# Matmuls grouped by tile shape in a three-stage kernel, with the float64 conversion ending in GpSimd's add, four input buffers for it and a single decay buffer

## The chip, the core and the metric

The kernel runs on one core of a Trainium2 chip. The core has a matrix engine (TensorE, PE in the profile; PEld is its weight load), VectorE (DVE), ScalarE (ACT), GpSimd (POOL) and SyncE (SP), which here issues nearly all DMAs. Each engine takes its own instructions in their order and waits on semaphores for the others. The metric is device time in microseconds (us), the median of several runs.

## The reference

Three computations run one after the other. The first is a linear attention with decay, for 4 batches, 8 heads, 768 steps and a head size of 48:

```python
for t in range(S):
    cur = np.einsum('bhd,bhe->bhde', u[None] * kt, vt)
    y[:, :, t] = np.einsum('bhd,bhde->bhe', rt, state + cur)
    state = wt[:, :, :, None] * state + np.einsum('bhd,bhe->bhde', kt, vt)
```

Its output, as 3072 tokens of width 384, goes through a soft mixture of experts (8 experts of 4 slots, width 1024). That takes a softmax of `x @ phi` over the tokens to fill the slots, two matmuls with a relu between them in each expert, and a softmax over the slots to hand the results back. The last part is bilinear:

```python
a = x @ w_a
b = x @ w_b
return (a * b @ w_out).astype(np.float32)
```

The three matrices `w_a`, `w_b` (384x1536) and `w_out` (1536x384) are float64, and the kernel turns them into float32 itself. The inputs r, k, v, w, u, phi, w1 and w2 are float32.

## The kernel before, in words

**Units.** The attention is cut into chunks of 128 steps. A unit is three chunks of four heads (two pairs of heads), and there are 16 units (`NU`). A unit n has three parts, each a generator. `front` turns w, k and r so that the head dimension lies on the partitions (PE transposes, L508, and ACT copies, L513 and L515). It forms the running products of the decays forwards (`decays`, a DVE scan, L532) and backwards (`backward`, L537), sums up decays over 1 for a later range check (`over`, ACT, L546), and multiplies them into k and r (`key` on GpSimd, L551; `query` on DVE, L555; `own` on GpSimd, L558). `mid` forms the scores within a chunk (`scores`, L581, one call for a head pair p and a head hh of it, masked by DVE at L584), turns the keys back (`keys`, L592), and forms the state updates (`updates`, L600 on PE, L605 to L611 on DVE), the states (GpSimd, L621) and the bonus term. `out` adds up in PSUM (the matmul accumulators, in banks) what the earlier chunks' state gives (L674, 128x128 weights) and what the scores give (L678, weights of 128x64), and DVE adds the bonus (L683).

**What sets the order.** The order is written by the program. `run_all` interleaves generators: each yields a share of its planned time, and the one that is furthest behind its plan goes next. In round n it interleaves `mid(n)`, `front(n + 1)`, `out(n - 1)`, half a token group of the experts' softmax (`moe.group`), a piece of the float64 conversion (`convert`) and one to two loads of expert weights. `MIDS` and `FRONTS` are lists of steps with their shares. Every engine then runs its own part in that order.

**Conversion.** 36 pieces of 128x384 float64 are loaded as pairs of 32-bit words into `cv_raw` buffers (three of them before). ACT turns both words of a piece into partial results (`stage`, L706 and L707), DVE shifts the upper one (L714), GpSimd adds the lower one as integers (L717), and DVE merges the sign, which it takes from the raw upper word (L720). The load three pieces on goes into the same buffer and waits for that.

**Buffers and queues.** The natural-order inputs have fixed buffers: w two, k and r one, v three. A load of the next unit's data is issued by SP when the last reader has its turn in the program. For w that is `over`. Score tiles are taken from the same ring of five PSUM banks as transposes and updates (`TPB`, tag `tp`). SP issues its DMAs in order, and each waits for a free one of eight semaphores as well as for the readers of its buffer.

**After the units** the experts run (L806, L831), for which 16 weight tiles are loaded: 4 early, the others into buffers that the attention gives back. Then come the bilinear part as products of slot pairs (L966) and the output (L1101, L1104).

The functions that the diff touches and what calls them:

## Time and profile before

| what | value |
|---|---|
| median of 3 runs | 411.43 us (408.06 to 414.76) |
| the profiled execution's own time | 412.5 us |
| its span, from the first to the last instruction | 410.8 us |
| mean granted TensorE clock over the span | 0.935 of full speed |
| units (first forward scan to the end of the last `out`) | 7.7 to about 268 us |
| experts, waiting for their weights | about 275 to 302 us |
| bilinear part and output | about 306 to 410 us |

The profile is of one execution. PE rows are matmuls, which are pipelined, so a row's length includes its fill and drain, and the distance from one row's start to the next tells more than its length. A float32 matmul stands as two instructions, a transpose as one. Tile shapes stand as rows*columns of the weights: 64*128 uses half of the array's rows, 128*64 half of its columns.

### The profile page before, as it was taken

How to read it: one execution, taken by the hardware profiler on the slowest of the kernel's cores; microseconds unless marked ns; L12 is line 12 of the kernel's file. 1: busy time of each engine (PE TensorE's matmuls, PEld its weight loads, DVE VectorE, ACT ScalarE, POOL GpSimd, SP SyncE). 2: the span in 40 equal slices, each digit the busy share in tenths (PEclk: the TensorE clock that was granted, in tenths of full speed). 3: DMA queues.
4: the chain of work that ended last, by engine and by line, in shares of the span. 5: the costliest groups of instructions: out<-in, count | busy, mean ns of one | idle time of the engine just before them, and what ended most of it. 6: DMA issues, size and time to landing. Idle time of an engine off the chain costs nothing.

```text
span 410.8 us, 9983 instructions
## 1 busy us (share of the span) xinstructions
PE 383.2 (93%) x3634; PEld 300.3 (73%) x3634; DVE 305.3 (74%) x616; ACT 233.9 (57%) x672; POOL 182.2 (44%) x225
## 2 busy tenths in 40 slices
...
GB/s 139 144 199 153 171 134 204 205 132 230 221 137 193 183 166 193 201 195 145 151 186 98 123 274 282 167 307 375 375 128 219 102 0 0 164 295 291 135 99 65
...
## 3 DMA queue, kind: packets, MB, share of 16 engines
...
q8 instruction: 31, 0.51, 0.5%
...
## 4 chain that ended last, share of the span: by engine, by line
PE 31%; DVE 9%; DMA 8%; issue 4%; ACT 2%; POOL 1%; SPq 1%; ACTq 0%; POOLq 0%; DVEq 0%
DMA s<-in_moe_w_dram 6%; PE yo L1101 5%; PE tp L581 4%; PE y L678 3%; PE yo L1104 3%; PE tp L966 3%; PE y L674 3%; PE tp L508 2%; DMA out_dram<-s 2%; DVE s L532 1%; PE tp L203 1%; DVE s L941 1%; PE tp L600 1%; DVE s L952 1%; PE misc L214 1%
## 5 line engine op out<-in xcount | busy, mean ns | idle before, releaser
L581 PE MATMUL tp<-s,s 64*128 64x128 f32 x384 | 64.9, 306 | 0.4 <-DVE s L611 0.3
L581 PEld LDWEIGHTS tp<-s,s 64*128 64x128 f32 x384 | 52.0, 203 | 9.1 <-issue 2.0
L508 PE MATMUL tp<-ident,s 128*128 128x128 f32 x288 | 52.2, 304 | 4.4 <-ACT s L513 3.2
L584 DVE TENSOR_TENSOR s<-tp,s 128x384 f32<-128x384 f32 x64 | 35.1, 549 | 19.9 <-PE tp L581 19.6
L551 POOL TENSOR_TENSOR s<-s,s 128x384 f32<-128x384 f32 x30 | 38.7, 1308 | 17.4 <-DVE s L537 14.8
L648 ACT ACTIVATE s<-s,s 128x48 f32<-128x48 f32 x192 | 46.2, 323 | 0.3
L678 PE MATMUL y<-s,s 128*64 128x48 f32 x768 | 44.8, 241 | 0.0
L508 PEld LDWEIGHTS tp<-ident,s 128*128 128x128 f32 x288 | 35.0, 152 | 12.8 <-ACT s L513 3.5
L558 POOL TENSOR_TENSOR s<-s,s 128x384 f32<-128x384 f32 x32 | 35.5, 1128 | 17.9 <-DVE s L555 17.9
L532 DVE TENSOR_TENSOR_SCAN s<-s,s 128x387 f32<-128x387 f32 x32 | 38.4, 1240 | 6.4 <-ACT s L513 6.4
L678 PEld LDWEIGHTS y<-s,s 128*64 128x64 f32 x768 | 32.5, 146 | 12.7 <-issue 6.0
L717 POOL TENSOR_TENSOR wab<-wab,s 128x384 int32<-128x384 int32 x24 | 28.5, 1188 | 25.0 <-issue 7.3
L1101 PE MATMUL yo<-s,s 128*128 128x384 f32 x192 | 37.8, 338 | 0.5 <-DVE s L1066 0.4
L966 PE MATMUL tp<-s,s 128*128 128x384 f32 x144 | 29.8, 358 | 5.2 <-DVE s L952 4.4
L1101 PEld LDWEIGHTS yo<-s,s 128*128 128x128 f32 x192 | 33.8, 188 | 1.2 <-DVE s L1066 1.1
L515 ACT ACTIVATE s<-tp 128x384 f32<-128x384 f32 x64 | 30.7, 491 | 5.8 <-PE tp L508 5.2
L966 PEld LDWEIGHTS tp<-s,s 128*128 128x128 f32 x144 | 26.0, 198 | 9.9 <-DVE s L952 6.9
L674 PE MATMUL y<-s,s 128*128 128x96 f32 x128 | 30.4, 321 | 0.0
L537 DVE TENSOR_TENSOR_SCAN s<-s,s 128x387 f32<-128x387 f32 x32 | 29.1, 952 | 0.5
L1108 ACT ACTIVATE s<-yo 128x384 f32<-128x384 f32 x24 | 11.8, 492 | 28.1 <-PE yo L1105 14.8
L621 POOL TENSOR_TENSOR s<-s,pc_all 64x288 f32<-64x288 f32 (+1 forms) x32 | 20.5, 640 | 14.1 <-DVE s L611 12.9
L674 PEld LDWEIGHTS y<-s,s 128*128 128x128 f32 x128 | 20.5, 201 | 7.7 <-issue 4.1
...
## 6 DMA issues: line engine op xcount, KB each, us to landing
...
s<-in_w_dram SPq DMA_DIRECT2D x48, 96.0 KB, 2.9
s<-in_k_dram SPq DMA_DIRECT2D x48, 96.0 KB, 3.2
s<-in_r_dram SPq DMA_DIRECT2D x48, 96.0 KB, 2.9
s<-in_v_dram SPq DMA_DIRECT2D x48, 96.0 KB, 3.3
...
```

The costliest lines, as they stand in the source:

```text
L508: nc.tensor.transpose(out=pt[:, c, :], in_=t[:, c, 2 * p:2 * p + 2, :].rearrange("p h d -> p (h d)"), identity=ident)
L515: nc.scalar.activation(out=(kT if nm == "k" else rT)[:, off:off + 3 * C], in_=pt.rearrange("p c s -> p (c s)"), func=ACTF.Copy)
L532: nc.vector.tensor_tensor_scan(out=P[:, hs[p]], data0=wt[:, hs[p]], data1=self.lo, initial=0.0, op0=ALU.mult, op1=ALU.max)
L551: (nc.gpsimd if n else nc.vector).tensor_tensor(out=part(suf, p, 1), in0=part(suf, p, 1), in1=plain(kT, p), op=ALU.mult)
L558: nc.gpsimd.tensor_tensor(out=plain(rT, p), in0=plain(rT, p), in1=plain(kT, p), op=ALU.mult)
L581: nc.tensor.matmul(out=ap_[:, c, :], lhsT=K[64 * hh:64 * hh + 64, o + 1:o + 1 + C], rhs=R[64 * hh:64 * hh + 64, o:o + C], start=True, stop ...
L584: nc.vector.tensor_tensor(out=a, in0=ap_, in1=self.mask.unsqueeze(1).to_broadcast([128, 3, C]), op=ALU.mult)
L648: nc.scalar.activation(out=av[:, c, h], in_=V[:, c, h, 0:D], func=ACTF.Copy, scale=a0[:, c, h // 2, h % 2:h % 2 + 1])
L674: nc.tensor.matmul(out=yp[:, c].rearrange("p h d -> p (h d)"), lhsT=R[:, o:o + C], rhs=self.sbd[q][:, p, (j + 2) % 3, :], start=True, stop ...
L678: nc.tensor.matmul(out=yp[th, c, hh, :], lhsT=am[p, hh][:, c, th], rhs=V[:, c, 2 * p + hh, :], start=j == 0, stop=j == 0 or hh == 1)
L966: nc.tensor.matmul(out=tp[m], lhsT=a[:, m * 128:(m + 1) * 128], rhs=b, start=first and i == 0, stop=last and i == 2)
L1101: nc.tensor.matmul(out=y, lhsT=a[:, m, :], rhs=self.th[:, m, :], start=m == 0 and a is fh, stop=False)
```

## The change

The diff makes these edits:

1. `scores` takes a pair of heads at once: two PSUM tiles, and the six matmuls alternate between the heads, whose operands lie on partitions 0 to 63 and 64 to 127. The two masks follow.
2. `out` issues the state's matmuls of both head pairs first (both PSUM tiles are open at once), then twelve score matmuls for each pair in one row.
3. `MIDS` puts the two `keys` together and the two `updates` together, and shifts shares.
4. The conversion: DVE first cuts the raw upper word to its sign bit in place, then shifts and merges the sign in one instruction, and GpSimd's integer add is last. `stage` runs one piece further ahead. There are four raw buffers, and the load into one waits for GpSimd's add.
5. w has one buffer, `over` writes in place, and loads w for the next unit (before: the one after the next). The buffer set free is the fourth raw buffer.
6. A branch that the constant `YDVE` had switched off is gone.

```diff
-YDVE = 1
-MIDS = (('keys', (0,), 327), ('scores', (0, 0), 654), ('bonus_t', (), 440), ('keys', (1,), 327),
-        ('scores', (0, 1), 654), ('updates', (0,), 474), ('scores', (1, 0), 0), ('bonus', (), 95),
-        ('updates', (1,), 544), ('av', (0,), 257), ('states', (), 0), ('av', (1,), 327), ('scores',
-        (1, 1), 0), ('av', (3,), 327), ('av', (2,), 327))
+MIDS = (('keys', (0,), 0), ('keys', (1,), 400), ('scores', (0,), 900), ('bonus_t', (), 700), ('updates', (0,), 0),
+        ('updates', (1,), 1018), ('bonus', (), 95), ('scores', (1,), 654), ('av', (0,), 257), ('states', (), 0),
+        ('av', (1,), 327), ('av', (3,), 327), ('av', (2,), 327))
...
-        for nm, nb in (("w", 2), ("k", 1), ("r", 1), ("v", 3)):
+        for nm, nb in (("w", 1), ("k", 1), ("r", 1), ("v", 3)):
...
-        self.load("w", 1)
...
         def over():
-            t = rT.bitcast(BF16)[:, 0:12 * 64]
-            nc.scalar.activation(out=t, in_=self.nat["w"][n % 2].rearrange("p c h d -> p (c h d)"),
-                                 func=ACTF.Relu, bias=self.neg1, accum_out=self.wover[:, n:n + 1])
-            self.load("w", n + 2)
+            t = self.nat["w"][0].rearrange("p c h d -> p (c h) d")[:, :, 0:self.sh.D]
+            nc.scalar.activation(out=t, in_=t, func=ACTF.Relu, bias=self.neg1, accum_out=self.wover[:, n:n + 1])
+            self.load("w", n + 1)
...
-        def scores(p, hh):
-            ap_ = ps_a.tile([128, 3, C], F32, tag="A", name="ap_")
+        def scores(p):
+
+            aps = [ps_a.tile([128, 3, C], F32, tag="A", name="ap_") for hh in range(2)]
             for c in range(3):
                 o = (p * 3 + c) * (C + 1)
-                nc.tensor.matmul(out=ap_[:, c, :], lhsT=K[64 * hh:64 * hh + 64, o + 1:o + 1 + C],
-                                 rhs=R[64 * hh:64 * hh + 64, o:o + C], start=True, stop=True)
...
+                for hh in range(2):
+                    nc.tensor.matmul(out=aps[hh][:, c, :], lhsT=K[64 * hh:64 * hh + 64, o + 1:o + 1 + C],
+                                     rhs=R[64 * hh:64 * hh + 64, o:o + C], start=True, stop=True)
...
+        yps = [ps_y.tile([128, 3, 2, D], F32, tag="y", name="yp") for p in range(2)]
+        cs = [c for c in range(3) if hf * 3 + c]
         for p in range(2):
-            yp = ps_y.tile([128, 3, 2, D], F32, tag="y", name="yp")
+            for c in cs:
+                o = (p * 3 + c) * (C + 1)
+                nc.tensor.matmul(out=yps[p][:, c].rearrange("p h d -> p (h d)"), lhsT=R[:, o:o + C],
+                                 rhs=self.sbd[q][:, p, (hf * 3 + c + 2) % 3, :], start=c == cs[0], stop=False)
+        yield 1084
+        for p in range(2):
+            yp = yps[p]
             for c in range(3):
...
                 for hh in range(2):
                     for th in (slice(0, 64), slice(64, 128)):
                         nc.tensor.matmul(out=yp[th, c, hh, :], lhsT=am[p, hh][:, c, th],
-                                         rhs=V[:, c, 2 * p + hh, :], start=j == 0, stop=j == 0 or hh == 1)
-                yield 542
+                                         rhs=V[:, c, 2 * p + hh, :], start=False, stop=c == 2 and hh == 1)
...
-def f64_to_f32(nc, out, raw, ahead):
-
-
-    bits = out.bitcast(I32)
-    nc.vector.tensor_scalar(out=out.bitcast(U32), in0=out.bitcast(U32), scalar1=3, scalar2=None,
-                            op0=ALU.logical_shift_left)
+def f64_to_f32(nc, out, raw):
+
+
+    bits = out.bitcast(U32)
+    nc.vector.tensor_scalar(out=raw[:, :, 1], in0=raw[:, :, 1], scalar1=0x80000000, scalar2=None, op0=ALU.bitwise_and)
     yield 1
-    nc.gpsimd.tensor_tensor(out=bits, in0=bits, in1=raw[:, :, 0].bitcast(I32), op=ALU.add)
-    ahead()
-    yield 2
-    nc.vector.scalar_tensor_tensor(out=out.bitcast(U32), in0=raw[:, :, 1], scalar=0x80000000, in1=out.bitcast(U32),
-                                   op0=ALU.bitwise_and, op1=ALU.bitwise_or)
+    nc.vector.scalar_tensor_tensor(out=bits, in0=bits, scalar=3, in1=raw[:, :, 1], op0=ALU.logical_shift_left,
+                                   op1=ALU.bitwise_or)
+    yield 1
+    nc.gpsimd.tensor_tensor(out=out.bitcast(I32), in0=out.bitcast(I32), in1=raw[:, :, 0].bitcast(I32), op=ALU.add)
     yield 1
```

**On PE, in the second half of a unit.** Names: `tp`, `y` and `misc` are PSUM tiles, `s_6_92` and the like are areas of on-chip memory, and the line numbers of the changed kernel are 1 to 3 lower at these places (L581 becomes L579, L600 becomes L599, L678 becomes L680). Before, the scores of a head and the pieces of `out` stand between other steps:

```order
L581 MATMUL tp_1460<-s_6_92,s_4_85 128x128 x3
L674 MATMUL y_1411<-s_6_92,s_4_86 128x96
L678 MATMUL y_1411<-s_4_87,s_8_95 64x48 x4
L508 MATMUL tp_1471<-ident,s_3_80 128x128 x3
L600 MATMUL tp_1486<-s_6_92,s_5_91 64x48 x6
L674 MATMUL y_1411<-s_6_92,s_4_86 128x96
L678 MATMUL y_1411<-s_4_87,s_8_95 64x48 x4
L581 MATMUL tp_1504<-s_6_92,s_4_85 128x128 x3
L639 MATMUL tp_1509<-ident,s_5_89 128x128
L640 MATMUL tp_1509<-ident,s_5_89 128x64
L600 MATMUL tp_1513<-s_6_92,s_5_91 64x48 x6
```

The same place in the changed kernel:

```order
L599 MATMUL tp_1458<-s_6_92,s_5_91 64x48 x6
L599 MATMUL tp_1467<-s_6_92,s_5_91 64x48 x6
L505 MATMUL tp_1476<-ident,s_3_80 128x128 x3
L680 MATMUL y_1411<-s_4_87,s_8_95 64x48 x12
L638 MATMUL tp_1507<-ident,s_5_89 128x128
L639 MATMUL tp_1507<-ident,s_5_89 128x64
L579 MATMUL tp_1512<-s_6_92,s_4_85 128x128
L579 MATMUL tp_1513<-s_6_92,s_4_85 128x128
L579 MATMUL tp_1512<-s_6_92,s_4_85 128x128
L579 MATMUL tp_1513<-s_6_92,s_4_85 128x128
L579 MATMUL tp_1512<-s_6_92,s_4_85 128x128
L579 MATMUL tp_1513<-s_6_92,s_4_85 128x128
```

Updates stand side by side, the score part of `out` is one row of twelve, and the two heads' score matmuls alternate between two PSUM tiles.

**On DVE, at the start of a unit.** Before, the shift of a piece stands ahead of the unit's forward scans (a scan is printed here as SCALAR_TENSOR_TENSOR of 128x387), and the sign of the piece behind the backward scans, with GpSimd's add between the two:

```order
L584 TENSOR_TENSOR s_8_94<-tp_2017,s_6_92 128x384
L714 TENSOR_SCALAR wo<-wo 128x384
L532 SCALAR_TENSOR_TENSOR s_3_82<-s_2_77,s_3_83 128x387 x2
L541 RECIPROCAL s_2_78<-s_3_82 128x6
L537 SCALAR_TENSOR_TENSOR s_4_85<-s_2_77,s_2_78 128x387 x2
L720 SCALAR_TENSOR_TENSOR wo<-s_1_73,wo 128x384
L584 TENSOR_TENSOR s_8_94<-tp_2094,s_6_92 128x384
```

In the changed kernel:

```order
L714 SCALAR_TENSOR_TENSOR wab_182<-wab_182,s_1_73 128x384
L266 SCALAR_TENSOR_TENSOR acc<-acc,s_7_93,misc_1949 96x384
L583 TENSOR_TENSOR s_8_94<-tp_2010,s_6_92 128x384
L583 TENSOR_TENSOR s_8_94<-tp_2011,s_6_92 128x384
L712 TENSOR_SCALAR s_1_74<-s_1_74 128x384
L529 SCALAR_TENSOR_TENSOR s_3_82<-s_2_77,s_3_83 128x387 x2
L714 SCALAR_TENSOR_TENSOR wab_182<-wab_182,s_1_74 128x384
L538 RECIPROCAL s_2_78<-s_3_82 128x6
L534 SCALAR_TENSOR_TENSOR s_4_85<-s_2_77,s_2_78 128x387 x2
```

Two masks now stand between a piece's last DVE step (L714), which GpSimd's add waits for, and the scans, and no DVE step stands behind that add.

**On SP, in the first half of a unit.** Before, the w buffers alternate (`s_1_72` here, `s_2_76` in the unit after), and a raw load, ahead of the k loads, waits for DVE:

```order
L727 DMA s_1_75<-in_moe_w_b_dram 128x768 [waits DMAHW5_49,DVE_49]
L492 DMA s_2_79<-in_k_dram 128x4x48 [waits DMAHW6_49,PE_49]
L492 DMA s_2_79<-in_k_dram 128x4x48 [waits DMAHW7_49,PE_49]
L492 DMA s_2_79<-in_k_dram 128x4x48 [waits DMAHW0_49,PE_49]
L307 DMA ct_176<-cstage 48x384 [waits DMAHW1_49,Activation_49]
L492 DMA s_1_72<-in_w_dram 128x4x48 [waits DMAHW2_49,Activation_49]
L492 DMA s_1_72<-in_w_dram 128x4x48 [waits DMAHW3_49]
L492 DMA s_1_72<-in_w_dram 128x4x48 [waits DMAHW4_49]
```

In the changed kernel:

```order
L723 DMA s_1_74<-in_moe_w_b_dram 128x768 [waits DMAHW1_49,Pool_49]
L773 DMA s_10_1170<-in_moe_w_dram 128x3x256 [waits DMAHW2_49]
L489 DMA s_2_79<-in_k_dram 128x4x48 [waits DMAHW3_49,PE_49]
L489 DMA s_2_79<-in_k_dram 128x4x48 [waits DMAHW4_49,PE_49]
L489 DMA s_2_79<-in_k_dram 128x4x48 [waits DMAHW5_49,PE_49]
L305 DMA ct_172<-cstage 48x384 [waits DMAHW6_49,Activation_49]
L489 DMA s_2_76<-in_w_dram 128x4x48 [waits DMAHW7_49,Activation_49]
L489 DMA s_2_76<-in_w_dram 128x4x48 [waits DMAHW0_49]
L489 DMA s_2_76<-in_w_dram 128x4x48 [waits DMAHW1_49]
```

The raw load waits for GpSimd, and the w loads, in the same place, are for the next unit.

## Rows read from the trace of the kernel before

**Rows 1.** The page, busy time of each engine over the span.

```profile
PE 383.2 (93%) x3634; PEld 300.3 (73%) x3634; DVE 305.3 (74%) x616; ACT 233.9 (57%) x672; POOL 182.2 (44%) x225
```

**Rows 2.** Windows of the span: length, busy time by engine, granted clock, DMA share, GB/s.

```profile
63.90:109.80 45.90, 45.28 (x521) 35.47 (x520) 41.23 (x88) 36.79 (x116) 30.20 (x31) 1.00 0.78 190
...
141.90:173.20 31.30, 30.61 (x350) 23.61 (x349) 29.30 (x63) 24.13 (x79) 20.44 (x21) 1.00 0.78 190
173.20:179.90 6.70, 5.71 (x60) 4.58 (x57) 6.63 (x10) 4.02 (x11) 4.38 (x4) 1.00 0.95 221
179.90:193.60 13.70, 13.09 (x78) 10.24 (x78) 10.16 (x26) 7.83 (x25) 7.02 (x8) 0.50 0.65 165
...
224.10:237.40 13.30, 13.22 (x147) 10.44 (x146) 10.31 (x24) 8.07 (x28) 6.40 (x7) 1.00 0.47 105
237.40:265.00 27.60, 27.60 (x333) 21.27 (x332) 17.18 (x48) 15.15 (x56) 7.15 (x11) 1.00 0.75 238
...
278.00:302.00 24.00, 24.00 (x298) 10.82 (x297) 9.92 (x26) 8.79 (x21) 0.51 (x1) 1.00 1.00 352
```

**Rows 3.** Timeline of PE within the units: start, length, operation, tile shape, count.

```profile
157.89 0.63 PE L629 MATMUL tp<-s,s 128*32 128x128 f32 x12
...
160.77 0.46 PE L674 MATMUL y<-s,s 128*128 128x96 f32 x2
161.17 0.44 PE L678 MATMUL y<-s,s 128*64 128x48 f32 x8
161.53 0.55 PE L508 MATMUL tp<-ident,s 128*128 128x128 f32 x3
162.01 0.56 PE L600 MATMUL tp<-s,s 128*64 128x48 f32 x12
...
163.60 0.93 PE L581 MATMUL tp<-s,s 64*128 64x128 f32 x6
164.47 0.33 PE L639 MATMUL tp<-ident,s 128*128 128x128 f32 x1
...
169.86 0.49 PE L508 MATMUL tp<-ident,s 128*128 128x128 f32 x3
...
171.14 0.88 PE L508 MATMUL tp<-ident,s 128*128 128x128 f32 x6
```

**Rows 4.** The chain that ended last, PE at 183 us: start, length, what.

```profile
183.43 1.58 PE tp L581 x6
```

**Rows 5.** Groups of DVE instructions by shape: count, busy, mean of one, idle before.

```profile
L532 DVE TENSOR_TENSOR_SCAN s<-s,s 128x387 f32<-128x387 f32 x32 | 38.4, 1240 | 6.4 <-ACT s L513 6.4
...
L720 DVE SCALAR_TENSOR_TENSOR wab<-s,wab 128x384 uint32<-128x384 uint32 x24 | 20.3, 845 | 6.8 <-POOL wab L717 5.1 <-DMA s<-in_moe_w_b_dram 1.4
...
L714 DVE TENSOR_SCALAR wab<-wab 128x384 uint32<-128x384 uint32 x24 | 11.2, 465 | 4.3 <-ACT wab L706 4.3
...
L720 DVE SCALAR_TENSOR_TENSOR wo<-s,wo 128x384 uint32<-128x384 uint32 x12 | 10.0, 831 | 1.9 <-POOL wo L717 1.9
```

**Rows 6.** Timeline of DVE at two units' starts.

```profile
141.93 2.60 DVE L532 TENSOR_TENSOR_SCAN s<-s,s 128x387 f32<-128x387 f32 x2
...
144.79 1.82 DVE L537 TENSOR_TENSOR_SCAN s<-s,s 128x387 f32<-128x387 f32 x2
...
156.93 0.56 DVE L720 SCALAR_TENSOR_TENSOR wab<-s,wab 128x384 uint32<-128x384 uint32 x1 [0.30 <-POOL wab L717]
...
173.22 2.58 DVE L532 TENSOR_TENSOR_SCAN s<-s,s 128x387 f32<-128x387 f32 x2
```

**Rows 7.** Timeline of GpSimd at the first of those starts.

```profile
142.15 1.55 POOL L717 TENSOR_TENSOR wab<-wab,s 128x384 int32<-128x384 int32 x1 [1.92 <-ACT s L513]
```

**Rows 8.** Timeline of SP's DMA issues within a unit.

```profile
161.96 1.99 SPq L492 DMA_DIRECT2D s<-in_w_dram  x3
```

**Rows 9.** DMA issues of 60 to 224 us: count, KB each, median us to landing.

```profile
s<-in_w_dram SPq DMA_DIRECT2D x30, 96.0 KB, 2.8
```

**Rows 10.** Waits of SP's queue: us in total, times, longest.

```profile
SPq L727 <- DVE s L683: 40.6, 11, 5.0
```

**Rows 11.** The chain that ended last, at the experts' weights.

```profile
278.26 8.00 DMA s<-in_moe_w_dram
```

More of the change, by code (lines that the diff above doesn't have):

```diff
@@ L412 @@
 class Chunked:
[L415 removed]
+    AREAS = (((("cv_raw", 768, 1),), (("cv_raw", 768, 1),), (("cv_raw", 768, 1),), (("cv_raw", 768, 1),)),
              ((("nat_w", 768, 1),), (("wt", 775, 1),), (("dl", 774, 1),), (("nat_k", 768, 1),)),
@@ L575, in mid @@
         kn = {}
-        def scores(p, hh):
-            ap_ = ps_a.tile([128, 3, C], F32, tag="A", name="ap_")
+        def scores(p):
+            aps = [ps_a.tile([128, 3, C], F32, tag="A", name="ap_") for hh in range(2)]
             for c in range(3):
                 o = (p * 3 + c) * (C + 1)
-                nc.tensor.matmul(out=ap_[:, c, :], lhsT=K[64 * hh:64 * hh + 64, o + 1:o + 1 + C],
-                                 rhs=R[64 * hh:64 * hh + 64, o:o + C], start=True, stop=True)
-            a = sb.tile([128, 3, C], F32, tag="am", name="am")
-            nc.vector.tensor_tensor(out=a, in0=ap_, in1=self.mask.unsqueeze(1).to_broadcast([128, 3, C]),
-                                    op=ALU.mult)
-            am[p, hh] = a
+                for hh in range(2):
+                    nc.tensor.matmul(out=aps[hh][:, c, :], lhsT=K[64 * hh:64 * hh + 64, o + 1:o + 1 + C],
+                                     rhs=R[64 * hh:64 * hh + 64, o:o + C], start=True, stop=True)
+            for hh in range(2):
+                a = sb.tile([128, 3, C], F32, tag="am", name="am")
+                nc.vector.tensor_tensor(out=a, in0=aps[hh], in1=self.mask.unsqueeze(1).to_broadcast([128, 3, C]),
+                                        op=ALU.mult)
+                am[p, hh] = a
         def keys(p):
```

34 lines of the change are left out of this document (12 added, 22 removed).

## The prediction

> **What bounds the kernel now.** I read the page's busy times first, then the windows by stage, then PE's timeline inside a unit, and last the groups of DVE, GpSimd and SP. The page has PE at 93% of the span and DVE at 74% [rows 1], which would make it a matter of PE alone. The windows say otherwise for the units. Five units at full clock (three from 63.9 us, two from 141.9 us; a unit counts from one pair of forward scans to the next, as from 141.93 on [rows 6]) take 77.2 us, with 75.89 us of PE and 70.53 us of DVE [rows 2]. That is 15.4 us per unit, PE 15.2, DVE 14.1. PE is the bound, and DVE comes only 1.1 us behind it. From 224.1 us on, where no conversion is left, PE is busy 13.22 of 13.30 us and then 27.60 of 27.60, with DVE at 10.31 and 17.18 [rows 2]: there PE is the bound alone. Behind that, from 278 to 302 us, the DMA engines are full (share 1.00, 352 GB/s [rows 2]), and the chain waits for expert weights [rows 11].
>
> A unit at reduced clock costs more: from 179.9 to 193.6 us the granted clock is 0.50 (1.2 of 2.4 GHz), PE is busy 13.09 of 13.70 us [rows 2], and six score instructions take 1.58 us [rows 4] where they take 0.93 at full clock [rows 3].
>
> **The change on PE, per unit.** All by starts and lengths of [rows 3].
> - Scores. Six instructions (three float32 matmuls of 64*128) take 0.87 us from their start at 163.60 to the next row's at 164.47, and there are four such groups. Afterwards two groups of twelve alternate between the halves of the rows. No row shows two row halves at once. The nearest are column tiles: twelve instructions of 128*32 with 128 columns take 0.63 us, where six of 64*128 with as many columns take 0.93, so small tiles of one shape do run side by side. If the halves do so too, twelve cost what six do, and 2 x 0.87 = 1.74 us go. If not, only what a group costs beyond its instructions goes: one more instruction of 128 columns costs 0.11 us (six transposes 0.88, three 0.55), so 0.87 - 6 x 0.11 = 0.21 twice, 0.42 us. I take 1.74, since the 128*32 row is the nearest in kind.
> - Score part of `out`. Eight instructions take 0.44 us and twelve (L600, same tile shape) 0.56, so one costs 0.03. A group of eight is 0.36 us from start to start (161.17 to 161.53); 24 are then 0.36 + 16 x 0.03 = 0.84. Six groups at 0.36 become two at 0.84: 0.48 us less.
> - State part of `out`. A lone pair is 0.40 us (160.77 to 161.17). A unit has six or four pairs, 2.40 or 1.60 us. In a row they are 0.40 + 10 x 0.11 = 1.50 or 0.40 + 6 x 0.11 = 1.06: 0.90 or 0.54 less, 0.72 on average.
> - The two updates side by side save one group's fixed part, 0.36 - 8 x 0.03 = 0.12 us. The keys save less than that and aren't counted.
>
> Together 3.06 us (1.74 without overlapping halves). PE falls from 15.2 to 12.1 us per unit (13.4). Either is below DVE's 14.1: in the units with conversion the next limit is DVE, and whether the halves overlap hardly matters there.
>
> **The change on DVE and GpSimd.** The counts stay: 36 pieces, each with two DVE steps and one add.
> - The wait of the sign step for GpSimd (5.1 + 1.9 = 7.0 us [rows 5]) goes, 0.5 us in each of 14 units. It is idle time, 0.5 of the 1.3 us per unit in which DVE is not busy. Some of the rest is waiting for PE; I leave 0.6.
> - The cut to the sign bit reads and writes every second word, where the shift (465 ns [rows 5]) was dense. No row shows this. Nearest below is that 465 ns; above, an unhindered two-input step over the same strided words, 0.56 us [rows 6]: 0 to 0.1 us per piece, 0.25 us per unit. I take 0, as it is the same operation with one input, and keep 0.25 for the range.
> - GpSimd's add and DVE's scans hinder each other. Two forward scans take 2.60 us where the two backward ones take 1.82 [rows 6], and GpSimd's add started at 142.15 us and ran for 1.55, in the middle of them [rows 7]. Over 32 scans the excess is 38.4 - 16 x 1.82 = 9.3 us [rows 5, 6], some 12 units of 0.78. In the new order two masks stand between the DVE step that releases the add and the scans, so this collision mostly goes; but the other conversion steps now lie at the scans of other units. I count half, 0.39 us per unit (ends 0 and 0.78).
>
> DVE then needs 14.1 - 0.4 = 13.7 us, and with 0.6 idle a unit lasts 14.3 instead of 15.4: 1.1 us less. GpSimd's add is now last, and on POOL's queue `key`, `own` and the states stand behind it; it has 9 to 10 us of work in 15.4 [rows 2], which covers this. If that cover fails, `key` is late, and the next unit's keys with it.
>
> *The shared port.* GpSimd's time (20.44 us in the two units from 141.9 [rows 2]) and the scans without hindrance (2 x 3.64 [rows 6]) and six sign steps at 0.56 add up to 31.1 of 31.3 us. The Trainium skill ("GPSIMD Engine Reference", Key points) says that GpSimd shares its SBUF interfaces with VectorE and is in contention with DVE instructions that have two SBUF inputs. The trace agrees in kind (2.60 against 1.82 us); how strictly no row tells, since GpSimd's lengths hold its own waiting. This is a rival below.
>
> **Loads of w.** They are issued from 161.96 to 163.95 us [rows 8], land 2.8 us later [rows 9], at 166.8, and are for the unit after next. Now the next unit needs them, whose w transposes start at 169.86 [rows 3]: 3.1 us to spare, 2.0 in a shorter unit. ACT's `over`, which the loads wait for, covers fewer elements. Cost 0 while that holds.
>
> **The sum.** From 63.9 to 224.1 us stand ten units, eight of them at full clock: 8 x 1.1 = 8.8 us. For the two at half clock, PE's saving counts 1.58 / 0.87 = 1.8 fold, some 2 us each after DVE's limit; PE's new waits will bring further falls of the clock, and I set the two against each other. At the start the second unit's w comes later (it was loaded at once), while two units at half clock gain: 0. Unit 14 (224.1 to 237.4) goes from 13.3 to DVE's 10.3 + 0.6: 2.4 us. The last stretch (27.6 us, all PE) holds one `mid` and two `out`s: 1.74 + 0.12 + 2 x 1.20 = 4.3 us. But the expert weights follow, and DMA was only 25% free in that stretch, so I count half, 2.1 us. In all 13.3 us. The profiled execution took 412.5 us, so 399.2; the median of the runs lies 1.1 us lower: **398 us**.
>
> **Rivals.**
> 1. *DVE is relieved altogether*: all collisions go, idle falls to 0.4. A unit is 14.1 - 0.78 + 0.4 = 13.7 us, 8 x 1.7, with 4 us from the slow-clock units, 2.4 and 4.3: 24 us, 387. For it: the masks now stand between. Against: GpSimd's `key` still falls on the backward scans. Chance 0.11.
> 2. *The shared port is the bound*: by the 31.1 of 31.3 us nothing is left in the units with conversion, and only the last 4.5 us are gained: 407. Against: DVE's stalls are already inside its 14.1 us. Chance 0.13.
> 3. *The clock falls more often*. It fell at 179.9 us, after a stretch in which PE was busy 5.71 of 6.70 us [rows 2], 85%; afterwards PE has 12.1 of 14.3, also 85%. A spell of 13.7 us at half clock does 7.6 us of the unit's 12.1, so that unit takes 13.7 + 4.5 = 18.2. If half of the eight get one, 4 x 3.9 = 15.6 us are lost again: 413. Against: in most units PE's waits lie apart. Chance 0.11. The Trainium skill ("TensorE: Matmul & The Clock Gate", HAM oscillation) says that gaps in PE's work bring the clock to half, and that each return is paid for; by that rule the time is this rival's, and the trace agrees at 179.9 us.
> 4. *Slower: w comes late.* SP issues in order; a raw load that waits for GpSimd's add stands ahead of the k and w loads. Such loads waited for DVE 11 times, 40.6 us in all, at most 5.0 [rows 10]. From a block of 3.1 us on, the unit is longer than before; with 5.0 the transposes start 3.0 us late in a unit of 14.3, 17.3 us: 8 x 1.8 = 14 us more, less the last 4.5: 422. Against: only some blocks stand ahead of w. Chance 0.10.
> 5. *The row halves don't overlap*, so the change does not do what it says. In the units DVE bounds anyway; the last units gain some 3 us less: 401. Chance 0.07.
>
> **How the numbers follow.** The forecast has 0.48 (391 to 405), the rest as above. About 2% either way, 8.2 us, is what a measurement of this kernel can tell from no change. Faster by over 2% (below 403.2): nine tenths of the forecast, rival 1, most of 5: 0.61. Slower by over 2%: most of 4 and some of 3, 0.11. Within: 0.28. The range 386 to 412 leaves out half of rival 1 and most of 3 and 4.
>
> **What would show it.** In the changed profile: starts of two score instructions of different halves within a few ns, and twelve in about 0.9 us; PE below 90% and DVE above 95% busy in the units; no DVE wait for the add; forward scan pairs near 1.82 us in most units; units of 14.3 us; no PE wait for w. I am wrong if the units keep 15.4 us with DVE below its limit, if PE waits for w or for GpSimd's `key`, or if the half clock covers more of the units than now.

## The result, and the profile after

The changed kernel takes **392.19 us** (median of 4 runs, 391.67 to 393.63), the kernel before 411.54 us (median of 4, 408.06 to 414.76). The ratio is **0.9537, 95% interval 0.9492 to 0.9582**: faster by 4.6%. The profiled execution took 391.77 us with a span of 390.0. Runs of one kernel with the old matmuls differ by some 2.6% among themselves, together with the granted clock; medians are of all runs, ratios of the undisturbed ones.

The page of the changed kernel, busy time of each engine, beside [rows 1]:

```profile
PE 336.3 (86%) x3634; PEld 265.6 (68%) x3634; DVE 308.2 (79%) x616; ACT 227.5 (58%) x672; POOL 181.2 (46%) x224
```

PE's busy time fell by 46.9 us, DVE's did not fall: it rose by 2.9. The windows of the changed kernel (length, then busy time by engine, granted clock, DMA share, GB/s), beside [rows 2]. The first five lines and the last two follow one another; the line of 60.60 to 207.10 holds ten units.

```profile
60.60:102.80 42.20, 37.08 (x499) 28.86 (x497) 41.40 (x86) 32.80 (x108) 29.94 (x31) 1.00 0.88 203
102.80:131.70 28.90, 24.68 (x326) 19.92 (x325) 28.43 (x59) 22.45 (x75) 17.38 (x21) 0.94 0.85 188
131.70:162.10 30.40, 26.64 (x331) 21.39 (x329) 28.79 (x61) 22.22 (x74) 20.78 (x21) 0.89 0.84 190
162.10:191.30 29.20, 24.91 (x328) 19.84 (x328) 28.68 (x60) 22.63 (x76) 17.41 (x21) 0.94 0.86 191
191.30:220.70 29.40, 25.32 (x328) 20.41 (x327) 28.74 (x62) 21.40 (x74) 20.84 (x21) 0.94 0.81 187
...
60.60:207.10 146.50, 126.49 (x1637) 101.01 (x1635) 142.79 (x296) 111.64 (x366) 95.59 (x103) 0.94 0.85 191
...
220.70:255.00 34.30, 29.50 (x413) 22.51 (x415) 21.16 (x67) 17.44 (x69) 7.17 (x12) 0.95 0.83 262
255.00:282.00 27.00, 27.00 (x346) 12.34 (x335) 10.89 (x30) 9.75 (x23) 0.73 (x2) 1.00 1.01 356
```

Over the ten units DVE is busy 142.79 of 146.50 us, 97%, and PE 126.49, 86%: DVE is the bound, PE waits. A unit lasts 14.65 us on average. The same ten units of the kernel before took 160.20 us, with 155.41 of PE, 142.64 of DVE and a clock of 0.94:

```profile
63.90:224.10 160.20, 155.41 (x1656) 122.10 (x1654) 142.64 (x299) 118.36 (x372) 100.56 (x105) 0.94 0.74 178
```

Where the 20.8 us of span came from, by the starts of the forward scans:

| stretch | before | after | gained | forecast |
|---|---|---|---|---|
| start to the fifth unit | 63.9 | 60.6 | 3.3 | 0 |
| ten units | 160.2 | 146.5 | 13.7 | 8.8 |
| unit 14 | 13.3 | 13.6 | -0.3 | 2.4 |
| rest | 173.4 | 169.3 | 4.1 | 2.1 |

PE's rows in two units of the changed kernel (start, length, operation, tile shape, count), beside [rows 3]:

```profile
163.73 0.91 PE L599 MATMUL tp<-s,s 128*64 128x48 f32 x24
164.57 0.55 PE L505 MATMUL tp<-ident,s 128*128 128x128 f32 x3
165.04 0.91 PE L680 MATMUL y<-s,s 128*64 128x48 f32 x24
165.88 0.33 PE L638 MATMUL tp<-ident,s 128*128 128x128 f32 x1
...
168.75 0.90 PE L579 MATMUL tp<-s,s 64*128 64x128 f32 x10 [2.06 <-DVE s L610]
...
174.19 0.94 PE L579 MATMUL tp<-s,s 64*128 64x128 f32 x12
175.06 0.88 PE L505 MATMUL tp<-ident,s 128*128 128x128 f32 x6
...
176.10 1.48 PE L672 MATMUL y<-s,s 128*128 128x96 f32 x12
177.50 0.63 PE L628 MATMUL tp<-s,s 128*32 128x128 f32 x12
```

Twelve score instructions take 0.87 us from their start to the next row's, what six took before: the row halves do run side by side. The score part of `out` takes 0.84 us per pair, as worked out, the state part 1.40 (worked out 1.50). And PE waits for DVE, 2.06 us up to 168.75.

DVE's groups of the changed kernel (count, busy, mean ns of one, idle before), beside [rows 5] and two more of the kernel before, which stand last (L537 is the backward scan, L555 is `query`):

```profile
L534 DVE TENSOR_TENSOR_SCAN s<-s,s 128x387 f32<-128x387 f32 x32 | 35.0, 1121 | 0.5
L529 DVE TENSOR_TENSOR_SCAN s<-s,s 128x387 f32<-128x387 f32 x32 | 33.1, 1072 | 7.0 <-ACT s L510 7.0
...
L712 DVE TENSOR_SCALAR s<-s 128x384 uint32<-128x384 uint32 x36 | 23.2, 644 | 2.9 <-ACT wab L704 2.9
L551 DVE TENSOR_TENSOR s<-s,s 128x384 f32<-128x384 f32 x32 | 20.2, 669 | 0.0
L714 DVE SCALAR_TENSOR_TENSOR wab<-wab,s 128x384 uint32<-128x384 uint32 x24 | 18.2, 760 | 0.1
...
L537 DVE TENSOR_TENSOR_SCAN s<-s,s 128x387 f32<-128x387 f32 x32 | 29.1, 952 | 0.5
L555 DVE TENSOR_TENSOR s<-s,s 128x384 f32<-128x384 f32 x32 | 17.4, 580 | 0.1
```

The forward scans (L529) fell from 38.4 to 33.1 us, but the backward ones (L534) rose from 29.1 to 35.0, `query` (L551) from 17.4 to 20.2, and the cut to the sign bit (L712) takes 644 ns on average where the shift took 465 (456 over all 36 pieces). DVE's wait for GpSimd's add is gone (0.1 us before L714).

### The profile page after: what moved, and what is told of

It reads as the page before. It is cut to its first block, busy times and chain, and to the rows that moved or that the text cites. A ratio compares the mean times of both kernels' runs of the same rounds, so it can differ in the third digit from the quotient of the medians.

```text
span 390.0 us, 9985 instructions
## 1 busy us (share of the span) xinstructions
PE 336.3 (86%) x3634; PEld 265.6 (68%) x3634; DVE 308.2 (79%) x616; ACT 227.5 (58%) x672; POOL 181.2 (46%) x224
## 4 chain that ended last, share of the span: by engine, by line
DVE 49%; PE 24%; DMA 13%; issue 6%; SPq 4%; ACT 3%; POOL 0%; DVEq 0%; ACTq 0%; POOLq 0%
DMA s<-in_moe_w_dram 8%; DVE s L534 8%; DVE s L529 7%; PE yo L1098 6%; DVE s L583 6%; DVE s L712 5%; DVE wab L714 4%; DVE s L551 3%; PE yo L1101 3%; SPq L489 3%; DVE wo L714 2%; PE tp L579 2%; DVE s L683 2%; PE tp L963 2%; PE y L680 2%
## 5 line engine op out<-in xcount | busy, mean ns | idle before, releaser
L505 PE MATMUL tp<-ident,s 128*128 128x128 f32 x288 | 50.0, 298 | 7.7 <-ACT s L593 3.8
L579 PE MATMUL tp<-s,s 64*128 64x128 f32 x384 | 37.2, 298 | 18.9 <-DVE s L610 9.5
L579 PEld LDWEIGHTS tp<-s,s 64*128 64x128 f32 x384 | 30.2, 197 | 24.0 <-issue 21.7
L554 POOL TENSOR_TENSOR s<-s,s 128x384 f32<-128x384 f32 x32 | 37.4, 1190 | 18.5 <-DVE s L551 18.5
L505 PEld LDWEIGHTS tp<-ident,s 128*128 128x128 f32 x288 | 33.5, 148 | 18.1 <-issue 6.0
L583 DVE TENSOR_TENSOR s<-tp,s 128x384 f32<-128x384 f32 x64 | 32.4, 545 | 9.4 <-PE tp L579 9.2
L529 DVE TENSOR_TENSOR_SCAN s<-s,s 128x387 f32<-128x387 f32 x32 | 33.1, 1072 | 7.0 <-ACT s L510 7.0
L534 DVE TENSOR_TENSOR_SCAN s<-s,s 128x387 f32<-128x387 f32 x32 | 35.0, 1121 | 0.5
L680 PEld LDWEIGHTS y<-s,s 128*64 128x64 f32 x768 | 29.0, 156 | 9.0 <-issue 8.7
L680 PE MATMUL y<-s,s 128*64 128x48 f32 x768 | 33.2, 243 | 0.0
L1106 POOL DMA_DIRECT2D out_dram<-s x18 | 9.9, 553 | 33.9 <-ACT s L1105 32.0
L712 DVE TENSOR_SCALAR s<-s 128x384 uint32<-128x384 uint32 x36 | 23.2, 644 | 2.9 <-ACT wab L704 2.9
```

The costliest lines, as they stand in the source:

```text
L505: nc.tensor.transpose(out=pt[:, c, :], in_=t[:, c, 2 * p:2 * p + 2, :].rearrange("p h d -> p (h d)"), identity=ident)
L529: nc.vector.tensor_tensor_scan(out=P[:, hs[p]], data0=wt[:, hs[p]], data1=self.lo, initial=0.0, op0=ALU.mult, op1=ALU.max)
L534: nc.vector.tensor_tensor_scan(out=suf[:, hs[p]][:, ::-1], data0=wt[:, o + 1:o + H + 1][:, ::-1], data1=d1[:, hs[p]][:, ::-1], initial=0.0 ...
L554: nc.gpsimd.tensor_tensor(out=plain(rT, p), in0=plain(rT, p), in1=plain(kT, p), op=ALU.mult)
L579: nc.tensor.matmul(out=aps[hh][:, c, :], lhsT=K[64 * hh:64 * hh + 64, o + 1:o + 1 + C], rhs=R[64 * hh:64 * hh + 64, o:o + C], start=True, ...
L583: nc.vector.tensor_tensor(out=a, in0=aps[hh], in1=self.mask.unsqueeze(1).to_broadcast([128, 3, C]), op=ALU.mult)
```

## The experiments

Each is compared with the kernel before, run on the same chip. The ten units are those from the fifth unit's first forward scan to the fifteenth's, in each kernel's own profile, in us. The experiments ran on several chips, on which the medians of the kernel before are up to 2.3 us apart, so a difference of that size between two experiments counts only where the traces show it too.

| kernel | median | ratio, 95% interval | ten units | PE | DVE | clock |
|---|---|---|---|---|---|---|
| before | 411.5 to 413.8 | | 160.2 | 155.4 | 142.6 | 0.94 |
| changed | 392.19 | 0.9537, 0.9492 to 0.9582 | 146.5 | 126.5 | 142.8 | 0.94 |
| grouping alone | 411.12 | 0.9971, 0.9903 to 1.0038 | 165.1 | 132.4 | 141.6 | 0.90 |
| conversion and buffers alone | 402.98 | 0.9855, 0.9766 to 0.9944 | 146.3 | 145.1 | 143.5 | 1.00 |
| heads in turn | 392.95 | 0.9610, 0.9498 to 0.9723 | 147.6 | 134.1 | 142.7 | 0.93 |
| no add | 376.80 | 0.9198, 0.9110 to 0.9285 | 134.8 | 121.7 | 130.4 | 0.96 |
| old order | 404.43 | 0.9815, 0.9763 to 0.9868 | 155.6 | 131.3 | 134.8 | 0.90 |
| sign a piece later | 402.97 | 0.9782, 0.9730 to 0.9834 | 154.4 | 131.2 | 141.3 | 0.90 |
| sign at the piece's end | 402.57 | 0.9747, 0.9669 to 0.9824 | 157.0 | 131.2 | 148.0 | 0.88 |
| the same, old matmuls | 416.38 | 1.0111, 1.0026 to 1.0196 | 157.9 | 152.3 | 144.7 | 0.95 |
| w early | 389.01 | 0.9457, 0.9408 to 0.9505 | 145.5 | 126.7 | 142.4 | 0.94 |
| sign by ScalarE | 380.36 | 0.9208, 0.9167 to 0.9249 | 138.5 | 123.4 | 130.0 | 0.98 |

**Grouping alone.** The functions `f64_to_f32`, `convert` and `over` and the w buffers are those of before:

```diff
-        for nm, nb in (("w", 1), ("k", 1), ("r", 1), ("v", 3)):
+        for nm, nb in (("w", 2), ("k", 1), ("r", 1), ("v", 3)):
...
-    nc.vector.scalar_tensor_tensor(out=bits, in0=bits, scalar=3, in1=raw[:, :, 1], op0=ALU.logical_shift_left,
-                                   op1=ALU.bitwise_or)
-    yield 1
-    nc.gpsimd.tensor_tensor(out=out.bitcast(I32), in0=out.bitcast(I32), in1=raw[:, :, 0].bitcast(I32), op=ALU.add)
+    nc.gpsimd.tensor_tensor(out=bits, in0=bits, in1=raw[:, :, 0].bitcast(I32), op=ALU.add)
+    ahead()
+    yield 2
+    nc.vector.scalar_tensor_tensor(out=out.bitcast(U32), in0=raw[:, :, 1], scalar=0x80000000, in1=out.bitcast(U32),
+                                   op0=ALU.bitwise_and, op1=ALU.bitwise_or)
```

> The changed kernel with the conversion, the w buffers and over() of before: only the grouping of matmuls (scores, out, MIDS) is left of the change. Theory (PE's grouping makes the gain, VectorE is the next limit): VectorE needs about 13.9 us per unit as before and still waits 0.5 us for GpSimd's add, so units of 14.6 to 15.0 us and a time of 391 to 399 us. Rival (the new order of the conversion carries at least half of the gain): 401 us or more.

The rival's side: 411.12 us, no gain that can be measured, although PE needs 23 us less in the ten units. Its waits of DVE from 60 to 224 us (us in total, times, longest):

```profile
DVE wab L720 <- POOL wab L717: 13.2, 11, 1.5
DVE wo L720 <- POOL wo L717: 6.2, 5, 1.5
```

and of ScalarE in the same stretch:

```profile
ACT wab L706 <- DMA s<-in_moe_w_b_dram: 9.5, 4, 2.9
ACT wo L706 <- DMA s<-in_moe_w_out_dram: 8.7, 4, 3.7
...
ACT wab L706 <- DMA s<-in_moe_w_a_dram: 1.9, 1, 1.9
```

DVE waits 19.4 us for the add (before, in the same stretch, 6.5), and ScalarE 20.1 us for raw loads (6.8), because there are three raw buffers. The second is the one that PE meets most. PE's longest waits of the same stretch:

```profile
PE tp L506 <- ACT s L595: 15.4, 5, 3.7
PE tp L581 <- ACT s L595: 11.2, 4, 4.1
```

L595 is ScalarE's copy of the turned keys. ScalarE takes its instructions in order, and each of these waits of PE (26.6 us in all) ends some 2 us after a wait of ScalarE for a raw load, as at 156.2 and 158.3 us. For DVE PE waits 5.6 us here. What PE gives up these waits take. My theory that the grouping makes the gain fell here.

**Conversion and buffers alone.** The other half of the diff, on the kernel before.

> The kernel before with the conversion, the four raw buffers, the single w buffer and over() of the changed kernel; matmuls as before. Theory: PE bounds the units at 15.2 us of work whatever VectorE does, so within 4 us of before, 408 to 416 us, on the slower side if the single w buffer holds up the first units. Rival (the conversion carries the gain): 403 us or less.

402.98 us, at the rival's edge, so the theory fell from this side too. Its ten units in one window (columns as above):

```profile
61.70:208.00 146.30, 145.06 (x1639) 114.34 (x1637) 143.48 (x296) 112.19 (x366) 100.32 (x103) 1.00 0.87 193
```

They are as short as the changed kernel's, at full clock throughout, with PE busy 99%. So the old matmuls need 14.5 us per unit, not 15.2. The trace is of the fastest of its five runs (396.75 us, mean clock 0.962). The others took 402.32 to 404.10 us, and no trace of them is kept: whether their units are as short is not shown.

Why the clock stays up in this trace is seen in the kernel before where it fell, at 118 us. DVE's timeline there (start, length, operation):

```profile
109.80 2.59 DVE L532 TENSOR_TENSOR_SCAN s<-s,s 128x387 f32<-128x387 f32 x2
...
112.66 1.82 DVE L537 TENSOR_TENSOR_SCAN s<-s,s 128x387 f32<-128x387 f32 x2
114.39 1.20 DVE L720 SCALAR_TENSOR_TENSOR wab<-s,wab 128x384 uint32<-128x384 uint32 x1
...
116.51 0.54 DVE L584 TENSOR_TENSOR s<-tp,s 128x384 f32<-128x384 f32 x1
```

PE's, of the same stretch:

```profile
115.23 0.27 PE L640 MATMUL tp<-ident,s 64*128 64x64 f32 x1
117.10 0.56 PE L600 MATMUL tp<-s,s 128*64 128x48 f32 x12 [1.60 <-DVE s L584]
```

And the windows before and behind:

```profile
111.70:118.50 6.80, 5.20 (x65) 3.62 (x67) 6.73 (x14) 3.96 (x12) 3.30 (x4) 1.00 0.82 184
118.50:125.30 6.80, 6.80 (x44) 5.63 (x43) 5.82 (x16) 4.87 (x18) 5.18 (x7) 0.50 0.68 169
```

The sign step needs 1.20 us beside `key` on GpSimd, behind forward scans of 2.59 us beside the add, so the mask comes late, PE waits 1.60 us for it, and the clock is 0.50 from 118.5 to 125.3 us. The fall at 179.9 us [rows 2] lies in such a wait, 1.60 us of L600 for L584 up to 180.5. A mask as late as this does not bring such a wait everywhere: in the unit of 141.9 us it starts 6.7 us after the scans too, and there PE, which is behind with its work, waits under 0.4 us. With the conversion alone, in the same unit as the one of 109.8 us, DVE has

```profile
104.97 1.80 DVE L531 TENSOR_TENSOR_SCAN s<-s,s 128x387 f32<-128x387 f32 x2
...
110.53 0.54 DVE L582 TENSOR_TENSOR s<-tp,s 128x384 f32<-128x384 f32 x1
```

The scans take 1.80 us, the mask starts 5.6 us after their start instead of 6.7, and PE's waits for masks are 1.2 us in all from 60 to 224 us. The Trainium skill ("TensorE: Matmul & The Clock Gate", HAM oscillation) says that gaps in PE's work bring the clock to half; the trace agrees at both places. Not every wait of this length is followed by a fall: in the changed kernel PE waits 1.96 us, and the clock stays at 1.00 up to 125.3 us.

```profile
109.38 0.90 PE L579 MATMUL tp<-s,s 64*128 64x128 f32 x10 [1.96 <-DVE s L610]
```

**Heads in turn.**

```diff
-            for c in range(3):
-                o = (p * 3 + c) * (C + 1)
-                for hh in range(2):
+            for hh in range(2):
+                for c in range(3):
+                    o = (p * 3 + c) * (C + 1)
                     nc.tensor.matmul(out=aps[hh][:, c, :], lhsT=K[64 * hh:64 * hh + 64, o + 1:o + 1 + C],
```

> The changed kernel, with the three score matmuls of one head and then the three of the other in place of the alternation; all else as in the changed kernel. Twelve score instructions should take about 1.5 us in place of 0.9, so PE has some 1.2 us per unit more, 13.8 of 14.5. Theory (VectorE bounds the units, PE only what is outside the conversion): 393 to 398 us. Rival (PE or the chain through the scores sets the units' length): 16 units by 1.2 us more, about 410 us.

As the theory has it: PE is busy 7.6 us longer in the ten units, twelve score instructions take 1.26 us (at 176.79 us) where they take 0.94 when they alternate, and the time is 392.95. The overlap of the row halves is real, and worth under 1 us here by the medians, less than two chips can tell apart.

**No add.** The line with GpSimd's add is taken out.

> The changed kernel without GpSimd's add in the conversion: the low words are left out, the 36 adds of 1.0 to 1.2 us are gone, and nothing else. VectorE's instructions that overlap such an add are longer by about 17 us in all in the changed kernel's profile. Theory (VectorE is the bound, and its collisions with GpSimd are part of that bound): its busy time falls by 15 to 20 us and the time by 10 to 15 us, to 377 to 382 us. Rival (units are bound by the chain between engines, not by VectorE's time): 388 us or more.

376.80 us. In the ten units (columns as above) DVE has the same instructions and 12.4 us less busy time, and the length falls by 11.7:

```profile
58.90:193.70 134.80, 121.65 (x1640) 97.62 (x1638) 130.37 (x295) 111.35 (x367) 65.21 (x75) 0.96 0.89 211
```

So in the changed kernel DVE is the bound, and some 12 us of its time in those units are what GpSimd's adds cost it. A step with one input is hit as well: in the changed kernel the cut to the sign bit has a mean of 644 ns and is as short as 0.34 us (at 163.86 us, where GpSimd has at most a copy of 0.24 us beside it); beside `own` (L554) it takes 0.79.

```profile
163.86 0.34 DVE L712 TENSOR_SCALAR s<-s 128x384 uint32<-128x384 uint32 x1
...
110.60 2.33 POOL L554 TENSOR_TENSOR s<-s,s 128x384 f32<-128x384 f32 x2 [0.50 <-DVE s L551]
111.28 0.79 DVE L712 TENSOR_SCALAR s<-s 128x384 uint32<-128x384 uint32 x1
```

The Trainium skill ("GPSIMD Engine Reference", Key points) says that GpSimd contends with DVE instructions in a 2-port perf mode or with two SBUF inputs. The scans and the last step of a piece have two inputs, and the trace agrees for them (a pair of scans takes 1.81 us or, beside GpSimd, 2.59, the last step 0.53 or 1.20); in which mode the cut runs no run here shows.

**Old order, and two tries to do without its wait.** On the changed kernel, with grouping, four raw buffers and one w buffer:

```diff
-    nc.vector.tensor_scalar(out=raw[:, :, 1], in0=raw[:, :, 1], scalar1=0x80000000, scalar2=None, op0=ALU.bitwise_and)
+    nc.vector.tensor_scalar(out=out.bitcast(U32), in0=out.bitcast(U32), scalar1=3, scalar2=None,
+                            op0=ALU.logical_shift_left)
     yield 1
-    nc.vector.scalar_tensor_tensor(out=bits, in0=bits, scalar=3, in1=raw[:, :, 1], op0=ALU.logical_shift_left,
-                                   op1=ALU.bitwise_or)
+    nc.gpsimd.tensor_tensor(out=bits, in0=bits, in1=raw[:, :, 0].bitcast(I32), op=ALU.add)
     yield 1
-    nc.gpsimd.tensor_tensor(out=out.bitcast(I32), in0=out.bitcast(I32), in1=raw[:, :, 0].bitcast(I32), op=ALU.add)
+    nc.vector.scalar_tensor_tensor(out=out.bitcast(U32), in0=raw[:, :, 1], scalar=0x80000000, in1=out.bitcast(U32),
+                                   op0=ALU.bitwise_and, op1=ALU.bitwise_or)
```

> The changed kernel (matmuls grouped, four raw buffers, one w buffer) with the conversion steps in the old order: shift, GpSimd's add, sign, so that VectorE waits for the add again. Theory, formed after the first four runs (VectorE's wait for the add is what holds grouped matmuls back, through the masks queued behind it): 404 to 413 us, as with the grouping alone. Rival (the fourth raw buffer and the loads make the difference): 390 to 396 us.

404.43 us: the ratio is 0.9815, against 0.9971 with the grouping alone and 0.9537 for the changed kernel (12.2 us less by the medians). ScalarE's waits for raw loads are gone, so the four buffers are worth about 1.5%; DVE waits for the add 16.8 us from 60 to 224 us. Next the sign is issued one piece later, behind the next piece's shift and add:

```diff
-        yield from f64_to_f32(nc, dst, raws.pop(0))
...
+        yield from f64_to_f32(nc, dst, raws[0])
+        if last:
+            sign(nc, *last)
...
+        last = dst, raws.pop(0)
```

> The run with grouped matmuls and the old order, but the sign of a piece is taken one piece later, behind the next piece's shift and add, by when the add is long done. Theory (only the wait counts, not the new order as such): VectorE waits for no add, 388 to 396 us. Rival (the new order itself, say by other collisions with GpSimd, makes the difference): 401 us or more.

The rival's number, 402.97, but not for its reason: DVE waits for no add, and ScalarE waits 19.9 us for raw loads, since a raw buffer is kept longer. One wait was exchanged for another. On the old matmuls:

> The kernel before with four raw buffers, one w buffer and the old order with the sign one piece later; matmuls as before. Theory (without the wait PE has no gaps, so that the clock falls less often): as the conversion alone, 395 to 405 us, with units of 14.5 us wherever the clock is full. Rival (PE bounds at 15.2 us per unit, so the wait is hidden): 409 us or more.

422.26 us, from 415.13 to 423.27: too far apart for a ratio, and I draw nothing from it. Then, as a change of the run with the old order, the shift at a piece's start and the sign at its end:

```diff
     nc.gpsimd.tensor_tensor(out=bits, in0=bits, in1=raw[:, :, 0].bitcast(I32), op=ALU.add)
-    yield 1
+    yield 3
     nc.vector.scalar_tensor_tensor(out=out.bitcast(U32), in0=raw[:, :, 1], scalar=0x80000000, in1=out.bitcast(U32),
                                    op0=ALU.bitwise_and, op1=ALU.bitwise_or)
-    yield 1
...
-        yield 1
         yield from f64_to_f32(nc, dst, raws.pop(0))
```

> The late sign put off by a whole piece kept the raw buffer too long: ScalarE, which stages the pieces in order, then waited 19.9 us for raw loads, about as long as VectorE had waited for the add. Here grouped matmuls, four raw buffers and the old order again, with the shift at a piece's start, the add a quarter later and the sign at its end, so that neither VectorE nor the loads should wait. Theory (a wait in the conversion, wherever it stands, holds the grouped units back; the order as such does not matter): no VectorE wait for the add over 3 us in all, no ScalarE wait for raw loads over 3 us, 390 to 396 us. Rival (the new order itself makes the difference): 401 us or more with these waits gone.

Both waits are nearly gone (3.3 us for the add, none for raw loads), and still 402.57 us: the theory that only the waits count fell. DVE's groups in this kernel:

```profile
L717 DVE SCALAR_TENSOR_TENSOR wab<-s,wab 128x384 uint32<-128x384 uint32 x24 | 23.5, 978 | 2.6 <-POOL wab L715 2.6
L712 DVE TENSOR_SCALAR wab<-wab 128x384 uint32<-128x384 uint32 x24 | 17.2, 715 | 5.9 <-ACT wab L704 5.9
```

Sign and shift now stand together behind the backward scans, where GpSimd has its two `key` (2.65 us from 129.95). There they take 1.20 and 1.11 us:

```profile
128.84 1.82 DVE L534 TENSOR_TENSOR_SCAN s<-s,s 128x387 f32<-128x387 f32 x2
130.57 1.20 DVE L717 SCALAR_TENSOR_TENSOR wab<-s,wab 128x384 uint32<-128x384 uint32 x1
131.69 1.11 DVE L712 TENSOR_SCALAR wab<-wab 128x384 uint32<-128x384 uint32 x1
```

DVE needs 148.0 us in the ten units, 5.2 more than in the changed kernel, and idles 9.0 instead of 3.7.

> The same conversion (old order, sign at the end of the piece) with the matmuls as before. Theory (PE, at 14.4 us of work per unit, follows the granted clock, which falls when PE has to wait): as the conversion alone, 395 to 405 us, the mean granted clock above 0.94. Rival (with the old matmuls the new order is needed): 409 us or more.

416.38 us, the rival's side. The loss against the kernel before is not in the ten units (157.9 us, before 160.2) but ahead of them: 68.4 us to the fifth unit, before 63.9. In the ten units PE waits for masks again, and the clock falls behind that (columns as in the windows above):

```profile
116.00:123.00 7.00, 5.52 (x70) 3.89 (x70) 6.96 (x15) 3.34 (x11) 4.72 (x4) 1.00 0.91 177
123.00:133.00 10.00, 10.00 (x52) 8.68 (x52) 7.09 (x17) 5.91 (x20) 4.60 (x7) 0.50 0.56 149
```

**w early.** The second unit's w is loaded at the start into the raw buffer that is needed last:

```diff
+        self.w1 = sb.tile([128, 3, 4, 64], F32, tag="cv_raw", name="cv_raw")
+        nc.gpsimd.memset(self.w1[:, :, :, D:], 1.0)
+        self.load("w", 1)
...
-            self.load("w", n + 1)
+            if n != 1:
+                self.load("w", n + 1 if n else 2)
```

> The changed kernel, with w of the second unit loaded at the start into the raw buffer that the conversion takes last, and w of the third unit at the first unit's over; all else the same. Theory (the single w buffer holds up the second unit by 3 to 4 us): its scans start at 15 to 16 us in place of 19.4 and the time falls by 2 to 4 us, to 388 to 390 us. Rival (the start is bound elsewhere, and what is gained is lost in the next units): 391 us or more.

389.01 us, 3.2 less than the changed kernel; the second unit's scans start at 16.5 us, not 19.4, and the fifth unit's at 58.3, not 60.6. It is faster than both kernels and computes all that they do.

**Sign by ScalarE.** On that kernel `stage` gets one more line, and DVE's cut goes:

```diff
+    nc.scalar.activation(out=raw[:, :, 1].bitcast(F32), in_=raw[:, :, 1].bitcast(F32), func=ACTF.Copy, scale=0.0)
...
-    nc.vector.tensor_scalar(out=raw[:, :, 1], in0=raw[:, :, 1], scalar1=0x80000000, scalar2=None, op0=ALU.bitwise_and)
```

> The kernel with the early w of the second unit, and the cut to the sign bit taken from VectorE: ScalarE writes the raw upper word times 0.0 in its place, which leaves a zero with the word's sign if ScalarE keeps the sign of a zero (otherwise the sign of the weights is left out). VectorE has 36 steps of 0.64 us less, ScalarE 36 of about 0.45 us more (it is busy 11 of 14.5 us per unit). Theory (VectorE is the bound of the units): its 1.65 us per unit less give units of 13.0 to 13.5 us and 371 to 380 us. Rival (ScalarE, or the chain between the engines, sets the units' length): 385 us or more.

380.17 us, ratio 0.9190 (0.9125 to 0.9255), and the sign of the weights was not kept. The ten units take 13.8 us each, not the 13.0 to 13.5 expected. Then with a bias of minus zero:

> The kernel with early w in which ScalarE makes the sign word by a product with 0.0, now with a bias of minus zero from memory in place of the built-in one: the run without it lost the sign, which an added plus zero explains. Expected if that is the cause: the sign is kept, nothing of the computation is left out, and the time is that of the run without it, 376 to 382 us; VectorE's 0.64 us steps stay away. Rival (ScalarE drops the sign of a zero in the product itself): the same time with the sign of the weights left out.

380.36 us, the sign not kept again, so neither is a version to keep. The time tells what it is worth to take the 36 cuts from DVE and give ScalarE a step for each: 8.7 us against the kernel with early w. DVE's busy time falls by 12.4 us in the ten units, their length by 7.0; ScalarE is now at 124.8 of 138.5 us, and no engine is above 94%. That the chain between the engines now sets the units' length follows from this only by exclusion; no run tests it.

## Why the prediction came out right, and where it did not

The time (398 forecast, 392 measured) and the new bound are right. The way there was right in part.

- **The path.** The sum takes PE's relief as what shortens the units, with 0.5 us per unit for DVE's wait and nothing for the raw loads. By it grouping alone should have had units of 14.6 to 15.0 us, as I wrote ahead of that run; it has 16.5 (165.1 / 10) and no gain. The waits that hold grouped matmuls back, PE's for ScalarE behind the raw loads and DVE's for the add, which grow to 26.6 and 19.4 us, are not in the sum. That the time came out is in this part luck: the change holds both halves.
- **PE's terms.** Each row has about its size: 0.87 us for twelve scores, 0.84 for the score part, 1.40 for the state part. The sum of 3.06 us is too large. The first four of the ten units have 662 matmul instructions and full clock both in the changed kernel and with the conversion alone (second line), and PE needs 2.2 us per unit less. Which term is short is not shown.

```profile
60.64:117.78 57.14, 49.22 (x662) 38.62 (x665) 56.13 (x119) 45.08 (x148) 38.39 (x42) 1.00 0.88 202
61.74:119.81 58.07, 58.07 (x662) 45.74 (x665) 56.99 (x118) 44.73 (x148) 39.16 (x42) 1.00 0.89 201
```

- **Overlapping halves** hardly matter in the units, as rival 5 said (392.95 without). Its 3 us in the last units did not come either: the rest takes 168.4 us without the overlap, 169.3 with it.
- **"PE is the bound" at 15.2 us per unit.** Mis-sized. The five units of [rows 2] hold 871 matmul instructions, 174 per unit; the conversion alone, at full clock, has 1639 in ten units, 164, and PE busy 14.5 us. The units are counted from scan to scan, and those in which the clock fell hold only 134 and 131 instructions; the five hold work left over from such units:

```profile
109.80:126.90 17.10, 15.50 (x134) 12.39 (x133) 15.18 (x33) 10.78 (x34) 10.04 (x11) 0.80 0.78 188
173.20:192.00 18.80, 17.20 (x131) 13.35 (x129) 15.19 (x33) 10.64 (x33) 10.03 (x11) 0.68 0.81 196
```

At full clock PE was 0.2 us per unit ahead of DVE's 14.3, not 1.1. What made a unit of before last 16.0 us on average was the lowered clock, and both of its falls stand at a wait of PE for a mask.

- **The two units at half clock**, which I set to zero, gave 6.6 of the 13.7 us: from 109.8 and from 173.2 us they lasted 17.1 and 18.8 us, together 35.9, against 29.3 for two units after. The eight others gave about 7.1, of 8.8; as they held what these two had left over, a part of that is the clock's as well. The clock is at half for 20.5 us of the ten units before (6.8 and 13.7) and for 17.1 after, in spells of 3.4, 6.8, 3.4 and 3.4. With PE at 12.4 us of work per unit (37.08 / 3 at full clock) a lowered clock costs less: two units at 0.89 take 15.2 us each, three at 1.00 take 14.1.
- **DVE relieved by half of its collisions, 13.7 us.** Wrong: 14.3. They moved from the forward scans to the backward scans, `query` and the cut. I had named this possibility and counted it too small. DVE's idle time came out lower, 0.37 us per unit instead of 0.6, so that the unit of 14.3 became 14.65.
- **The strided cut at 0 to 0.1 us a piece.** Alone it costs what the shift does (0.34 us), but it meets GpSimd more often: 0.19 us more on average, 6.7 us over 36 pieces (23.2 against 11.2 + 5.3). The other DVE step of a piece gave 2.8 of it back (30.3 us before [rows 5], 18.2 + 9.3 after).
- **Unit 14, 2.4 us.** Wrong: in the changed order it holds conversion pieces, before it held none, so DVE bounds it (28.74 of 29.40 us with the unit ahead of it).
- **The start, 0 us.** It gained 3.3 in spite of the single w buffer, which costs 3.2 of what it could have been (early w). In the units PE waits for w 0.4 us in all; rival 4 fell.
- **Rivals 2 and 3.** The collisions are a real part of the bound (the run with no add), but inside DVE's time, as the text against rival 2 said. The clock fell about as much as before (0.945 over the span, 0.935 before) without the price of rival 3.

Grouping alone gives nothing measurable (0.3%), conversion and buffers alone 1.5%, both 4.6%. The conversion and its buffers take the waits off PE, DVE and ScalarE; the grouping takes PE below DVE, so that a lowered clock costs less, and shortens the stretch without conversion (169.3 us from 220.7 on, where the conversion alone has 173.3 from 221.7 on). That both are needed is shown; how the new order's 12 us over the old one divide into the wait and the collisions is not, as each kernel without the wait got another cost.
